# Casting one PSUM bank in two halves, on ScalarE and on VectorE, in a recurrent attention kernel

## The chip, the cores and the metric

The kernel runs on one core of one Trainium2 chip. The metric is the device time of one execution in microseconds (us). The engines are written as the profile writes them: PE is TensorE (PEld its weight loads), ACT is ScalarE, DVE is VectorE, POOL is GpSimd, SP is SyncE.

## The reference

Two branches work on the same x (1 x 2048 x 512, bf16), and a gate mixes them.

```python
g = _sigmoid((x * gate_w).sum(-1, keepdims=True))
a = _A_ref(x, A_mem0, A_Wq, A_Wk, A_Wv, A_Wo, A_seg_len)   # recurrent attention
b = _B_ref(x, B_w1, B_b1, B_w2, B_b2)                      # layernorm, 512 -> 1376 gelu -> 512
return g * a + (1 - g) * b

# _A_ref: 64 segments of 32 tokens, 32 heads of 128, memory of M = 8 tokens
mem = mem0
for s in range(n_seg):
    h = jnp.concatenate([mem, xs], axis=1)                 # 8 + 32 tokens, xs is segment s of x
    q, k, v = (einsum of h with Wq, Wk, Wv)
    p = _softmax(where(mask, q k^T * Dh**-0.5, -1e9))
    o = jnp.einsum('bhqk,bhke->bhqe', p, v)
    o = jnp.einsum('bhte,hed->btd', o, Wo)                 # output projection
    mem = o[:, :M, :].copy()                               # memory of the next segment
    outs.append(o[:, M:, :])
```

The 64 segments are a chain: the first 8 rows of a segment's output projection are the memory that the next segment's q, k and v are made from.

## The kernel before, in words

The kernel has two stages. The first (up to about 110 us) computes the mixer branch b for all tokens, in blocks of 256, stores (1 - g) * b in DRAM, and loads the attention weights, which then stay in SBUF. The second is the loop over the 64 segments, `for s in range(nseg)`, which takes the rest of the time. It is written under a manual schedule: each engine executes its instructions in the order in which the Python code issues them, and the framework adds the semaphore waits that the data dependences ask for.

PSUM has eight banks, each a tile of 128 partitions x 512 f32: U0 to U3 for q and k, and later for the attention output; X1 and X2 for v and for side work; SbF and W for the scores. W serves three purposes in an iteration: half of the scores, then the output projection, then the transposed memory rows.

One iteration s does the following, in this order on PE.

1. Line 110 (`qk_unit`): q and k of the segment into U0 to U3, 64 matmuls from the 32 token columns in `hT`. ACT casts each bank to `Tb` (line 115), and DVE transposes it to `QT` or `KT` (line 119).
2. Lines 254 and 258: scores. Line 129 (`v_unit`): v into X1 and X2. ACT takes the exponentials (line 644) and casts v to `V` (lines 659 and 670). DVE normalises the memory columns (lines 651 and 652).
3. Lines 265 and 268: the sums of the other columns into SbF. DVE takes their reciprocal (line 588, in `recip_x`). Lines 278 and 283 (`av`): attention output into U0 to U3. ACT casts its memory columns to `UT` (line 680), and then the other columns to `XR` (line 583), which POOL normalises in the next iteration (lines 599 and 600).
4. `wo_pass`, the output projection: 32 matmuls of line 141 from `UT` and `Wo_sb` into bank W. Then a cast of W on ACT, line 607, to the bf16 tile `w`, one of 11 buffers of 128 x 512.
5. Line 246 (`mask_mm(0)`): a mask into SbF. Then two units of side work (`run(W3)`).
6. Line 691: four matmuls with `w` as weights, one for each 128 columns of it, which select the memory rows and transpose them; they write columns 0 to 31 of bank W. DVE casts the result to the next `hT` (line 692), and updates a running minimum, `rmin` (line 693). The next iteration starts from `hT`.

The side work is a generator, `side(T, si)`, from which the loop takes units with `run(n)`: q, k and v of the tokens left over from a 128-token tile (`left_qk`, `left_v`), their output projection (`wo_left`), the transpose of the next tile of x (`x_mm`, copied to `xT` by DVE at line 160), and the assembly of finished output rows (`out_sel`, lines 224, 226 and 230), which reads `w` of earlier segments. A few iterations at the start and at the end have little or no side work.

The last segment is finished after the loop. There `wo_pass` is called twice more, first for the segment before the last (pass 64, issued between the reciprocal of line 704 and the multiplies of lines 707 and 708), and then for the last one (pass 65, read by line 732). So there are 65 calls in all, and 63 of them feed line 691.

Of the kernel before, what the change touches and what calls it, by code (L numbers as in the profile page):

```python
# [27 lines left out]
def kernel(ctx, tc, A_x, A_mem0, A_Wq, A_Wk, A_Wv, A_Wo, A_seg_len, B_x, B_w1, B_b1, B_w2, B_b2, gate_w, out):  # L28
    nc = tc.nc
    P = 128  # L30
    _, S, Dm = A_x.shape
# [65 lines left out]
    W = lps.tile([P, 512], FP32)  # L97
# [39 lines left out]
    def wo_group(bk, U_, n):  # L137
        j, ih = HORD[n]
        for c in range(4):
            i = 4 * ih + c  # L140
            nc.tensor.matmul(bk[32 * c:32 * c + 32, :], lhsT=U_[:, j, i, :], rhs=Wo_sb[:, 4 * i + j, :],  # L141
                             start=(n == 0), stop=(n == NW - 1), tile_position=(0, 32 * c))
# [460 lines left out]
    def wo_pass(U_):  # L603
        for n in range(NW):
            wo_group(W, U_, n)
        w = cw.tile([P, Dm], BF16, tag="w", bufs=11, name="w")
        nc.scalar.copy(out=w[:], in_=W[:])  # L607
        return w

    W1, W2, W3 = 2, 2, 2  # L610
    for s in range(nseg):
# [71 lines left out]
        flush(dve_q, 9)  # L683
        prep_q(s + 1)
        w = wo_pass(UT[s % 2])
        if s >= 1:
            ws[s - 1] = w
# [15 lines left out]
    nc.gpsimd.memset(UL[T % 2][:, :, :, LEFT * si:seg], 0.0)  # L703
    nc.vector.reciprocal(out=R[:, nx], in_=SbF[:, 0:32 * NG])
    ws[s - 1] = wo_pass(UT[s % 2])
    Rr = R[:, nx].rearrange("p (i q) -> p i q", q=32)
    nc.vector.tensor_tensor(out=E[:, :, 16:48], in0=E[:, :, 16:48], in1=Rr, op=ALU.mult)
# [16 lines left out]
    nc.vector.tensor_scalar(out=good[:, 0:1], in0=tot[:, 0:1], scalar1=R_MIN, scalar2=None, op0=ALU.is_gt)  # L724
    nc.vector.tensor_scalar(out=good[:, 1:2], in0=tot[:, 1:2], scalar1=RSUM_MAX, scalar2=None, op0=ALU.is_lt)
    wf = wo_pass(UF)
    nc.tensor.matmul(X1[0:1, 0:1], lhsT=good[:, 0:1], rhs=good[:, 1:2], start=True, stop=True)
    bad = okp.tile([1, 1], I32)
# [131 lines left out]
```

## Time and profile before

| what | value |
|---|---|
| median of 3 runs | 828.18 us (827.88 to 828.75) |
| the profiled execution's own time | 827.84 us |
| span of the profile | 826.1 us |
| mean granted PE clock | 0.995 |
| PE busy | 787.2 us |
| ACT busy | 574.1 us |
| DVE busy | 434.8 us |
| POOL busy | 250.1 us |
| line 607, ACT, 65 casts of 128 x 512 | 38.1 us, 585 ns each |
| line 692, DVE, 63 casts of 128 x 32 | 12.1 us, 192 ns each |

The profile is of one execution. Its rows give a group of instructions by line, engine and operation, what it writes and reads (out<-in), and busy time, mean duration and the idle time of the engine ahead of it with what ended that. The view of the waits names who waited for whom, with the total in us, the number of times and the longest. The chain that ended last is followed back from the last instruction, at each step to what released it. Ends of matmuls are modelled, and a matmul row's length includes its way through the array, so successive rows overlap.

### The profile page before, as it was taken

How to read it: one execution, taken by the hardware profiler on the slowest of the kernel's cores; microseconds unless marked ns; L12 is line 12 of the kernel's file. 1: busy time of each engine (PE TensorE's matmuls, PEld its weight loads, DVE VectorE, ACT ScalarE, POOL GpSimd, SP SyncE). 2: the span in 40 equal slices, each digit the busy share in tenths (PEclk: the TensorE clock that was granted, in tenths of full speed). 3: DMA queues.
4: the chain of work that ended last, by engine and by line, in shares of the span. 5: the costliest groups of instructions: out<-in, count | busy, mean ns of one | idle time of the engine just before them, and what ended most of it. 6: DMA issues, size and time to landing. Idle time of an engine off the chain costs nothing.

```text
span 826.1 us, 41283 instructions
## 1 busy us (share of the span) xinstructions
PE 787.2 (95%) x18418; PEld 413.4 (50%) x18418; DVE 434.8 (53%) x1059; ACT 574.1 (70%) x1442; POOL 250.1 (30%) x377
## 2 busy tenths in 40 slices
PE   6898998999999999999999999999999999999997
PEld 4565644545454454544454545454544544454443
DVE  4764445455545455554555555545455555555554
ACT  4554676777777677767676777777676767677763
POOL 3000023333333333333323333333333333323331
PEclk9999999999999999999999999999999999999999
DMA  6995111212121221212121212122111212121111
GB/s 193 406 351 187 34 53 54 62 42 80 55 87 54 68 73 38 79 60 81 60 81 54 70 47 86 54 78 64 66 54 57 81 60 81 54 81 51 60 53 62
DMA packets 38952, 70.42 MB, mean 85 GB/s; under 512 B 3948, under 2 KB 29137, under 8 KB 37233
## 3 DMA queue, kind: packets, MB, share of 16 engines
q1 hardware_dynamic: 38720, 67.59, 23.9%
q8 instruction: 146, 2.39, 1.2%
q14 instruction: 38, 0.30, 0.1%
q0 software_dynamic: 48, 0.13, 0.1%
HBM read 59.06 MB, written 4.45 MB: 77 GB/s over the span
## 4 chain that ended last, share of the span: by engine, by line
PE 85%; ACT 6%; DMA 4%; DVE 2%; issue 1%; SPq 0%; POOL 0%; DVEq 0%; ACTq 0%; POOLq 0%
PE U L110 27%; PE X L129 16%; PE W L141 14%; PE X L110 6%; ACT w L607 5%; PE U L278 3%; PE U L461 3%; PE X L141 3%; DMA c_dr<-ct 3%; PE W L691 2%; PE SbF L455 2%; PE W L455 2%; PE SbF L254 1%; DMA w_sb<-in_B_w_dram 1%; PE U L265 1%
## 5 line engine op out<-in xcount | busy, mean ns | idle before, releaser
L115 ACT CAST Tb<-U 128x512 bf16<-128x512 f32 x258 | 188.6, 756 | 59.1 <-PE U L110 33.3
L599 POOL TENSOR_TENSOR UT<-XR,Rb 128x768 bf16<-128x768 bf16 x63 | 104.9, 1666 | 258.5 <-DMA Rb<-r_dr 212.0
L110 PEld LDWEIGHTS <-hT 128*32 128x32 bf16 x4096 | 103.6, 97 | 109.5 <-DVE hT L692 15.3
L129 PE MATMUL X<-Wv_sb,hT 128*32 128x512 bf16 x2048 | 134.8, 378 | 0.0
L110 PE MATMUL U<-Wq_sb,hT 128*32 128x512 bf16 x2048 | 132.9, 379 | 1.4 <-DVE hT L692 1.4
L110 PE MATMUL U<-Wk_sb,hT 128*32 128x512 bf16 x2048 | 132.7, 379 | 0.0
L119 DVE STREAM_TRANSPOSE QT<-Tb 128x256 f32<-128x256 f32 x128 | 57.0, 446 | 134.7 <-ACT Tb L115 129.6
L141 PE MATMUL W<-Wo_sb,UT 128*32 128x512 bf16 x2080 | 124.5, 380 | 1.2 <-ACT UT L680 1.2
L593 POOL TENSOR_TENSOR racc<-racc,R 128x320 f32<-128x320 f32 x63 | 54.6, 866 | 200.3 <-DVE R L588 196.2
L588 DVE RECIPROCAL R<-SbF 128x256 f32<-128x256 f32 x63 | 110.3, 1751 | 0.5 <-PE SbF L268 0.5
L141 PEld LDWEIGHTS <-UT 128*32 128x32 bf16 x2080 | 55.6, 96 | 56.3 <-issue 16.0
L692 DVE CAST hT<-W 128x32 bf16<-128x32 f32 x63 | 12.1, 192 | 129.7 <-PE W L691 124.9
L583 ACT CAST XR<-U 128x256 bf16<-128x256 f32 x252 | 78.6, 438 | 0.0
L119 DVE STREAM_TRANSPOSE KT<-Tb 128x256 f32<-128x256 f32 x128 | 56.8, 444 | 30.6 <-ACT Tb L115 30.3
L607 ACT CAST w<-W 128x512 bf16<-128x512 f32 x65 | 38.1, 585 | 48.0 <-PE W L141 48.0
L680 ACT CAST UT<-U 128x64 bf16<-128x64 f32 x252 | 35.3, 227 | 43.4 <-PE U L283 43.4
L651 DVE RECIPROCAL R<-U 128x32 f32<-128x32 f32 x126 | 45.0, 357 | 23.2 <-PE U L268 19.0
L129 PEld LDWEIGHTS <-hT 128*32 128x32 bf16 x2048 | 45.1, 95 | 20.8
L461 PE MATMUL U<-w_sb,hTm 128*128 128x512 bf16 (+1 forms) x176 | 53.9, 391 | 1.3 <-DMA w_sb<-in_B_w_dram 1.3
L115 ACT CAST Tb<-X 128x512 bf16<-128x512 f32 x62 | 46.4, 748 | 10.8 <-PE X L110 10.7
L455 PEld LDWEIGHTS <-w_sb 128*128 128x128 bf16 (+1 forms) x352 | 35.3, 104 | 31.1 <-issue 13.6
L265 PEld LDWEIGHTS <-BO 128*32 128x32 bf16 x760 | 29.4, 94 | 34.6 <-issue 14.0
(146 smaller groups left out, 1190.9 us busy)
## 6 DMA issues: line engine op xcount, KB each, us to landing
Rb<-r_dr SPq DMA_DIRECT2D x63, 512.0 KB
Wq_sb<-in_A_Wq_dram SPq DMA_DIRECT2D x4, 1024.0 KB
Wk_sb<-in_A_Wk_dram SPq DMA_DIRECT2D x4, 1024.0 KB
Wv_sb<-in_A_Wv_dram SPq DMA_DIRECT2D x4, 1024.0 KB
Wo_sb<-in_A_Wo_dram SPq DMA_DIRECT2D x4, 1024.0 KB
VP<-VL SPq DMA_DIRECT2D x64, 64.0 KB
xt<-in_A_x_dram SPq DMA_DIRECT2D x16, 128.0 KB
c_dr<-ct SPq DMA_DIRECT2D x16, 128.0 KB
```

The lines of the kernel that those rows point to most:

```text
L110: nc.tensor.matmul(bk[32 * j:32 * j + 32, :], lhsT=G[:, kc, :], rhs=W5[t][:, kc, h0:h1, j, :], start=(kc == 0), stop=(kc == KC - 1), tile_ ...
L115: nc.scalar.copy(out=Tb[:].rearrange("p a e b -> p a b e"), in_=bk.rearrange("p (a b e) -> p a b e", a=8, b=2))
L119: nc.vector.transpose(out=dst[:, 8 * hf:8 * hf + 8, 0:32, :].rearrange("p a r b -> p a (r b)").bitcast(FP32), in_=Tb[:].rearrange("p a e b ...
L129: nc.tensor.matmul(bk[32 * j:32 * j + 32, :], lhsT=G[:, kc, :], rhs=Wv5[:, kc, 4 * vb:4 * vb + 4, j, :], start=(kc == 0), stop=(kc == KC - ...
L141: nc.tensor.matmul(bk[32 * c:32 * c + 32, :], lhsT=U_[:, j, i, :], rhs=Wo_sb[:, 4 * i + j, :], start=(n == 0), stop=(n == NW - 1), tile_po ...
L455: nc.tensor.matmul(hp[:rows, 0:TB * P], lhsT=w1_sb[:, kc, fc * P:fc * P + rows], rhs=yTs[blk][:, kc, :], start=(kc == 0), stop=(kc == KC - 1))
L461: nc.tensor.matmul(bp(blk, tt)[:], lhsT=hTm[blk % 2][:rows, fc, tt * P:(tt + 1) * P], rhs=w2_sb[:rows, fc, :], start=(fc == 0), stop=(fc = ...
L583: nc.scalar.copy(out=XR[:, j], in_=U[j][:, 0:NG * 40].rearrange("p (i q) -> p i q", q=40)[:, :, 8:40])
L588: nc.vector.reciprocal(out=R[:, 8 * NG:], in_=SbF[:, 0:32 * NG])
L593: nc.gpsimd.tensor_tensor(out=racc[:], in0=racc[:], in1=R[:], op=ALU.add)
L599: nc.gpsimd.tensor_tensor(out=UT[(s + 1) % 2][:].rearrange("p j i q -> p (j i) q")[:, :, M:32], in0=XR[:, :, 0:RIDE], in1=Rb[:, :, 0:RIDE] ...
L607: nc.scalar.copy(out=w[:], in_=W[:])
```

## The change

In `wo_pass`, the cast of W to `w` is written as two casts: ACT takes columns 0 to 255, and DVE columns 256 to 511. All 65 passes are concerned. In the changed kernel the second cast is line 608, and all later lines move down by one (691 becomes 692, 692 becomes 693, 707 becomes 708).

```diff
@@ -604,7 +604,8 @@
         for n in range(NW):
             wo_group(W, U_, n)
         w = cw.tile([P, Dm], BF16, tag="w", bufs=11, name="w")
-        nc.scalar.copy(out=w[:], in_=W[:])
+        nc.scalar.copy(out=w[:, 0:Dm // 2], in_=W[:, 0:Dm // 2])
+        nc.vector.tensor_copy(out=w[:, Dm // 2:Dm], in_=W[:, Dm // 2:Dm])
         return w
```

## Prediction

> **What bounds the kernel now.** I read the page first: which engine fills the span, and what the chain that ended last is made of.
>
> ```profile
> span 826.1 us, 41283 instructions
> PE 787.2 (95%) x18418; PEld 413.4 (50%) x18418; DVE 434.8 (53%) x1059; ACT 574.1 (70%) x1442; POOL 250.1 (30%) x377
> ...
> PE 85%; ACT 6%; DMA 4%; DVE 2%; issue 1%; SPq 0%; POOL 0%; DVEq 0%; ACTq 0%; POOLq 0%
> ```
>
> TensorE is the bound: 95% busy and 85% of the chain. The next share, ACT's 6%, is almost wholly the cast that is changed (ACT w L607 alone has 5% in the chain's lines). Then the waits, to see how much of that cast TensorE really stands still for:
>
> ```profile
> DVE hT L692 <- PE W L691: 124.9, 61, 2.3
> PEld L691 <- ACT w L607: 42.1, 63, 1.0
> PE W L691 <- ACT w L607: 11.3, 62, 0.6
> PE U L110 <- DVE hT L692: 1.4, 5, 0.4
> ```
>
> The columns are total us, times, longest. TensorE's matmuls wait for w in every iteration, 11.3 us in all, some 0.16 us each and 0.59 in three iterations that have no other work to put there. This is the largest wait that TensorE has in the loop. VectorE waits for those matmuls about 2 us each time, so it has nothing to do while w is cast. Last, the timeline of one iteration around the cast (start, length, engine; idle before in brackets):
>
> ```profile
> 417.72 0.28 PE L246 MATMUL SbF<-Mk,ident 128*32 128x224 bf16 x4
> ...
> 417.82 0.62 PE L129 MATMUL X<-Wv_sb,GL 128*32 128x512 bf16 x8
> 417.96 0.58 ACT L607 CAST w<-W 128x512 bf16<-128x512 f32 x1 [0.75 <-PE W L141]
> ...
> 418.60 0.25 PE L691 MATMUL W<-SelM,w 128*128 128x8 bf16 x4 [0.16 <-ACT w L607]
> ...
> 418.78 0.62 PE L129 MATMUL X<-Wv_sb,GL 128*32 128x512 bf16 x8
> 418.96 0.19 DVE L692 CAST hT<-W 128x32 bf16<-128x32 f32 x1 [2.16 <-PE W L691]
> 419.06 0.48 DVE L693 TENSOR_TENSOR rmin<-rmin,R 128x320 f32<-128x320 f32 x1
> ```
>
> TensorE covers most of the cast with mask and side matmuls, which end at 418.44, and then stands until 418.60. So a shorter cast can win at most the 0.16 us, 11.3 us over all; a longer one is paid in full, since nothing is left in TensorE's queue to run ahead of L691.
>
> **The wait that the change adds.** The order of the built program shows no instruction moved on TensorE and one added on VectorE: the second half (line 608 there) stands between the reciprocal (in one iteration of four, the copy to xT) and the cast to hT. What it waits for decides the case: not TensorE's last product in W, but ACT's semaphore, at just the count that ACT's own half raises. And the four matmuls of L691 now wait for VectorE, the first of them too: they write bank W, which the second half reads. So the halves do not run side by side; they stand in a row, each with its fixed time, and a hand-over is added.
>
> No row of this trace has the two engines reading one bank at once. At the end of the run they read different banks at once, and run at full pace:
>
> ```profile
> 816.41 0.65 ACT L712 CAST UT<-U 128x256 bf16<-128x256 f32 x2 [0.23 <-PE U L283]
> 816.46 0.76 DVE L712 CAST UT<-U 128x256 bf16<-128x256 f32 x2 [0.56 <-PE U L283]
> ```
>
> Beside this row, the Trainium skill (PSUM — Partial Sum Buffer, the section "PSUM bank collisions raise a hardware error") says that ScalarE and VectorE must be kept apart by a semaphore even when both only read the same bank and different columns of it; W is a single bank of 512 f32 columns. The same page's "Specifications (TRN2)" says that the two read in parallel at full bandwidth where the banks differ, which the row above bears out. By the second sentence alone the sum would be that of the first rival below; by the first it is the sum that follows.
>
> **The cost of a pass.** The L712 rows are the same operation at the halves' size: ACT 372 and 378 ns (375), VectorE 415 and 425 (420), against 585 for the whole cast on ACT (all 65 within 1 ns). The hand-overs are medians over the trace, from the end of one to the start of the other: TensorE's W to ACT 46 ns, ACT to VectorE 32 (Tb to its transpose), VectorE to a waiting matmul 56 (L254), ACT to the matmul 56 (L691).
>
> Before, from the end of W to the first L691: 46 + 585 + 56 = 687 ns. After: 46 + 375 + 32 + 420 + 56 = 929. So 242 ns more, all behind the last matmul that TensorE can do, and its wait grows from 0.16 to about 0.40 us.
>
> Bounds: ACT's half is at most 459 (the longest L583, same size, queued behind others), and 312 if only its pitch counts (four L583 in 1.25 us). VectorE's half is between 345 (start to start of the two L712) and 446 (mean of L119 at this width). Together that is +104 to +352 ns. I take the L712 values, since that row matches in operation, size and types, and since L691 starts 56 ns after the recorded end of w although ACT's next cast began 0.1 us before that end: a hand-over counts from the end, not from the pitch.
>
> Is VectorE free? In all 65 casts, no VectorE instruction of the trace lies in the stretch where the half would run. Behind its wait stand only the cast to hT, which needs L691 anyway, and rmin, which nobody awaits soon. POOL does run there, for 0.1 to 0.2 us mostly; L230, also VectorE out of f32 PSUM, takes 708 to 710 with POOL beside it for most of its length, so I charge nothing. ACT is free 0.21 us earlier, which is worth next to nothing: for its other casts of the loop, UT and V, TensorE waits 1.2 and 1.0 us in the whole run. No DMA, POOL or SP instruction moves.
>
> 63 passes with L691: 63 x 0.242 = 15.2 us.
>
> **The two passes at the end.** Pass 64's cast on ACT starts at 815.59, off the path. But its second half now stands in VectorE's queue ahead of the two multiplies L707 and L708, which ran at 814.80 and 815.15 and are on the chain. The half runs from 815.59 + 0.375 + 0.032 = 816.00; L707 follows 0.345 later, at 816.34, and takes 0.425; L278's first 16 matmuls follow at 816.82 and take 0.20, so L283 starts at 817.02 instead of 815.95: +1.07. (L708 no longer sets it: POOL's L718, beside which it took 753, is over by 815.82, and L652, its like, takes 226.) Pass 65 is on the chain up to L732: +0.24.
>
> **Sum.** 15.2 + 1.1 + 0.2 = 16.6 us against the profiled execution's own 827.84 (span 826.1 and 1.7 around it): 844.4. The median of the runs is 828.18, 0.3 higher, so I say 844.5, 2.0% slower.
>
> **Rivals.** First, **side by side**: VectorE's half starts from TensorE's last product, as its name says. Then W to VectorE 105 ns (L691 to L692) + 420 + 56 = 581 instead of 687: 0.106 less a pass, all inside TensorE's 0.16, so 63 x 0.106 = 6.7 us won; pass 64's half would still delay L707, by some 0.9 less 0.2 that L283 waits already. That makes 828.2 - 6.7 + 0.7 = about 822. For it: the overlap of the L712 rows. Against it: the wait in the built program. It decides only if that wait is over before ACT's half is, and the count says it isn't. 3%.
>
> Second, **the halves overlap in their tails**: if the pitches count, +0.104 a pass, 63 x 0.104 = 6.6 and about 1 at the end: 836. For it: ACT's casts start 0.1 us before the recorded end of the one ahead. Against it: that is inside one engine, while all hand-overs between engines in the trace come after the end. 8%.
>
> Third, **VectorE's half is slowed by POOL**: beside POOL's long operations L652 took up to 812 ns instead of 226. If one pass in four lost 0.53 (753 - 226, as L708 did), 16 x 0.53 = 8.5 more: 853. Against it: L652 and L708 read bf16 in SBUF; L230, out of PSUM, wasn't touched. 5%.
>
> **How the numbers follow.** The forecast, in a row with full hand-overs, has 84%. Its own range is 840 to 850: below, a quarter of the 15.2 us taken back elsewhere in the loop; above, nearly the upper bounds of both halves (63 x 0.352 + 1.4 = 23.6 us, 851.8). That leaves 16% out, so the range is this one. A change under 0.2% (1.7 us) is about what a measurement of this kernel cannot tell from none. Faster: the first rival, 3%. Same: 2%, the low edge of the second. Slower: 95%.
>
> **What would show it.** In the new profile: w twice, near 375 ns on ACT and 420 on VectorE, 65 times each; the VectorE half waiting for "ACT w", not for "PE W"; TensorE's wait at the four matmuls near 0.40 us a pass, 26 us in all, with VectorE's w as releaser; VectorE's w in the chain; L707's twin 1.5 us later. Wrong would be: the two casts with nearly equal starts; a half of over 500 ns; a wait of 0.40 with a total that rises by less than 12 us, which would mean that the loop takes it back.

## The result, and the profile after

The changed kernel takes 842.74 us in the median of four runs (841.41 to 843.62), against 828.34 before. The ratio is 1.0173, with a 95% interval of 1.0155 to 1.0190: slower by 14.4 us. The profiled execution took 843.19 us, 15.35 more than that of before. The ratios here and below are estimates over the runs in the faster of two states, and differ from the quotient of the two medians by 0.14% at most; one run of before, beside the last experiment, took 1533 us and is not in its ratio.

The page of the changed kernel: span, engines, chain by engine, and the groups of the two casts (busy, mean ns of one | idle of the engine ahead, with what ended it).

```profile
span 841.4 us, 41257 instructions
PE 780.9 (93%) x18390; PEld 421.4 (50%) x18418; DVE 459.7 (55%) x1124; ACT 559.9 (67%) x1442; POOL 249.7 (30%) x377
...
PE 85%; ACT 5%; DVE 4%; DMA 3%; issue 2%; SPq 0%; POOL 0%; ACTq 0%; DVEq 0%; POOLq 0%
...
L608 DVE CAST w<-W 128x256 bf16<-128x256 f32 x65 | 27.6, 425 | 94.4 <-ACT w L607 94.4
...
L607 ACT CAST w<-W 128x256 bf16<-128x256 f32 x65 | 24.2, 372 | 48.1 <-PE W L141 48.1
```

ACT is relieved: 574.1 us busy before, 559.9 now. But in the row of VectorE's half the engine idles until "ACT w", in all 65 passes, and the chain has lost one point of ACT and gained two of DVE. The waits of the changed kernel (us in all, times, longest):

```profile
DVE w L608 <- ACT w L607: 94.4, 65, 1.8
...
PE W L692 <- DVE w L608: 20.7, 48, 0.8
...
PEld L110 <- DVE hT L693: 11.4, 47, 0.4
...
PE W L692 <- ACT VL L194: 6.0, 15, 0.4
```

TensorE's idle time at the four matmuls is 20.7 + 6.0 = 26.7 us, where before had 11.3. Fifteen of these waits carry the name of ACT's cast VL: that cast ends within 0.03 us of VectorE's half, and the view names the latest. The first matmul waits for VectorE's semaphore alone. The timeline of one iteration:

```profile
434.26 0.62 PE L110 MATMUL X<-Wk_sb,GL 128*32 128x512 bf16 x8
434.39 0.37 ACT L607 CAST w<-W 128x256 bf16<-128x256 f32 x1 [0.65 <-PE W L141]
...
434.80 0.42 DVE L608 CAST w<-W 128x256 bf16<-128x256 f32 x1 [1.46 <-ACT w L607]
...
435.28 0.24 PE L692 MATMUL W<-SelM,w 128*128 128x8 bf16 x4 [0.40 <-DVE w L608]
```

ACT's half ends at 434.76, VectorE's starts at 434.80 and ends at 435.22, and the matmuls start at 435.28. One after the other, each with its whole length.

### The profile page after: what moved, and what is told of

The parts are those of the page before. It is cut to its first block, busy times and chain, and to the rows that moved or that the text cites. A ratio compares the mean times of both kernels' runs of the same rounds, so it can differ in the third digit from the quotient of the medians.

```text
span 841.4 us, 41257 instructions
## 1 busy us (share of the span) xinstructions
PE 780.9 (93%) x18390; PEld 421.4 (50%) x18418; DVE 459.7 (55%) x1124; ACT 559.9 (67%) x1442; POOL 249.7 (30%) x377
## 4 chain that ended last, share of the span: by engine, by line
PE 85%; ACT 5%; DVE 4%; DMA 3%; issue 2%; SPq 0%; POOL 0%; ACTq 0%; DVEq 0%; POOLq 0%
PE U L110 26%; PE X L129 16%; PE W L141 14%; PE X L110 6%; PE U L278 3%; PE U L461 3%; PE X L141 3%; DVE w L608 3%; ACT w L607 2%; PE W L692 2%; PE SbF L455 2%; PE W L455 2%; DMA c_dr<-ct 1%; PE SbF L254 1%; DMA w_sb<-in_B_w_dram 1%
## 5 line engine op out<-in xcount | busy, mean ns | idle before, releaser
L110 PEld LDWEIGHTS <-hT 128*32 128x32 bf16 x4096 | 106.7, 97 | 105.5 <-DVE hT L693 11.4
L608 DVE CAST w<-W 128x256 bf16<-128x256 f32 x65 | 27.6, 425 | 94.4 <-ACT w L607 94.4
L607 ACT CAST w<-W 128x256 bf16<-128x256 f32 x65 | 24.2, 372 | 48.1 <-PE W L141 48.1
L129 PEld LDWEIGHTS <-hT 128*32 128x32 bf16 x2048 | 45.1, 95 | 20.7
L461 PE MATMUL U<-w_sb,hTm 128*128 128x512 bf16 (+1 forms) x164 | 51.3, 391 | 1.9 <-DMA w_sb<-in_B_w_dram 1.3
```

What stands on the lines that cost most here:

```text
L110: nc.tensor.matmul(bk[32 * j:32 * j + 32, :], lhsT=G[:, kc, :], rhs=W5[t][:, kc, h0:h1, j, :], start=(kc == 0), stop=(kc == KC - 1), tile_ ...
L129: nc.tensor.matmul(bk[32 * j:32 * j + 32, :], lhsT=G[:, kc, :], rhs=Wv5[:, kc, 4 * vb:4 * vb + 4, j, :], start=(kc == 0), stop=(kc == KC - ...
L461: nc.tensor.matmul(bp(blk, tt)[:], lhsT=hTm[blk % 2][:rows, fc, tt * P:(tt + 1) * P], rhs=w2_sb[:rows, fc, :], start=(fc == 0), stop=(fc = ...
L608: nc.vector.tensor_copy(out=w[:, Dm // 2:Dm], in_=W[:, Dm // 2:Dm])
```

## The experiments

Eleven kernels tell the causes apart. Each was compared with the kernel before on the same chip; the median of before there is given, since chips differ by a microsecond or two. "End of W to the first matmul" is measured in the records of the trace, as the median over 63 passes: 687 ns before, 929 in the changed kernel.

**Both halves on ACT.**

```diff
-        nc.scalar.copy(out=w[:], in_=W[:])
+        nc.scalar.copy(out=w[:, 0:Dm // 2], in_=W[:, 0:Dm // 2])
+        nc.scalar.copy(out=w[:, Dm // 2:Dm], in_=W[:, Dm // 2:Dm])
```

> Both halves of W are cast by ACT, one after the other; VectorE is not in it. Theory (the loss is two casts in a row, each paid from its start to its recorded end, with a hand-over between engines): inside one engine the second cast starts before the recorded end of the first (two L712 casts on ACT took 0.65 us together), so from the end of W to the first matmul 46 + 650 + 56 = 752 ns against 687 before and 929 after; +0.065 us a pass, 63 passes, 4 us: about 832 us. Rival A (splitting as such is what costs, each piece with its full 0.37 us): 46 + 372 + 372 + 56 = 846 ns, +10 us: about 838 us. Rival B (nothing but VectorE's presence costs): 687 ns, 828 us.

Measured: 831.59 us against 829.72, ratio 1.0021 (1.0007 to 1.0034). End of W to the first matmul: 745 ns, where 752 was expected and rival A had 846. The casts take 372 and 378 ns, but the second starts 0.27 us after the start of the first. Splitting inside one engine costs 0.058 us a pass, a quarter of what the change costs.

**The whole cast on VectorE** (`nc.vector.tensor_copy(out=w[:], in_=W[:])`).

> The whole of W is cast by VectorE in one piece; ACT is not in it. Theory: one cast, no hand-over between engines in the middle. VectorE took 425 ns for 256 columns and 192 for 32, so 691 for 512; 105 + 691 + 56 = 852 ns from the end of W to the first matmul, 77 less than with the two halves, though VectorE is the slower engine: +0.165 us a pass, 10.4 us, less some 1 us that came back after the matmuls in the changed kernel, and 1.1 us at the end as there: 838 to 839 us, faster than the changed kernel's 842.7. Rival (VectorE's speed or its place in VectorE's queue is the cause, and ACT's half helps): slower than the changed kernel, 845 us or more.

Measured: 839.85 us against 829.72, ratio 1.0108 (1.0082 to 1.0133); 863 ns to the first matmul, where 852 was expected. The cast's row, duration min/median/max:

```profile
L607 DVE CAST w<-W x65: 690/692/692, 118.6 to 832.1; 128x512 bf16<-128x512 f32 x65
```

VectorE alone is 107 ns slower than ACT alone at this cast, and yet faster than ACT and VectorE together by 66 ns. So VectorE's speed is not the cause; the row of two is.

**A small piece for VectorE.**

```diff
+        nc.scalar.copy(out=w[:, 0:448], in_=W[:, 0:448])
+        nc.vector.tensor_copy(out=w[:, 448:Dm], in_=W[:, 448:Dm])
```

> ACT casts 448 columns and VectorE the last 64. Theory (in a row): ACT 532 ns (585 less 64 columns at 0.83 ns each), hand-over 32, VectorE 225 (192 and 32 columns more at 1.04 ns), so 46 + 532 + 32 + 225 + 56 = 891 ns, 38 less than at half and half; 842.7 - 63 x 0.038 = about 840.3 us. Rival (side by side, the time is that of the longer piece): 46 + 532 + 56 = 634 ns, less than the 687 of before: 825 us. Rival (VectorE's time alone sets it): 200 ns less than at half and half, about 830 us.

Measured: 839.05 us against 829.72, ratio 1.0104 (1.0078 to 1.0130); 888 ns, where 891 was expected. Its casts and the wait between them:

```profile
L607 ACT CAST w<-W x65: 532/532/533, 119.1 to 831.3; 128x448 bf16<-128x448 f32 x65
...
L608 DVE CAST w<-W x65: 223/225/226, 119.7 to 831.9; 128x64 bf16<-128x64 f32 x65
...
  ACT w L607: 104.0, 65
```

VectorE's piece fell from 425 to 225 ns and ACT's rose from 372 to 532, and the pass became shorter by their sum, 41 ns. Side by side, ACT's 532 would have been a gain over 585. Most of the small piece is fixed time: 225 ns for 64 columns, where a column costs 1.04 ns.

**Division by partitions.** ACT casts partitions 0 to 63 and VectorE 64 to 127, so that the two pieces have only the bank in common.

> W is divided by partitions: ACT casts partitions 0 to 63, VectorE 64 to 127, each all 512 columns. The two pieces share the bank but no partition. Theory (the wait is set by the bank, whatever part of it is read): in a row, 46 + 585 + 32 + 691 + 56 = 1410 ns, +0.72 us a pass, 46 us: about 874 us. Rival (the wait is set where the two read the same partitions): side by side, 105 + 691 + 56 = 852 ns, about 839 us.

One run: 871.93 us against 829.72; 1409 ns to the first matmul, where 1410 was expected.

```profile
446.05 0.58 ACT L607 CAST w<-W 64x512 bf16<-64x512 f32 x1 [0.65 <-PE W L141]
446.66 0.69 DVE L608 CAST w<-W 64x512 bf16<-64x512 f32 x1 [1.66 <-ACT w L607]
447.41 0.17 PEld L692 LDWEIGHTS <-w 128*128 128x128 bf16 x4 [1.37 <-DVE w L608]
```

The framework's wait goes by the bank, whatever part of it is read (each bank is one tile in this kernel, so the runs do not tell the two apart). The Trainium skill (PSUM — Partial Sum Buffer, "PSUM bank collisions raise a hardware error") allows two engines at once in one bank where their 32-partition quadrants differ. The framework's guard is coarser than that, and whether the chip would have borne it was not tried: there is no run without the wait.

**Two banks, pieces side by side.** Columns 0 to 255 go to bank W and 256 to 511 to bank SbF, which is free once the reciprocal of line 588 has read it; the mask moves behind the four matmuls. Each `wo_half` is four matmuls of 256 columns.

```diff
         for n in range(NW):
-            wo_group(W, U_, n)
+            wo_half(W, U_, n, 0)
+            wo_half(SbF, U_, n, 1)
...
-        nc.scalar.copy(out=w[:], in_=W[:])
+        nc.scalar.copy(out=w[:, 0:Dm // 2], in_=W[:, 0:Dm // 2])
+        nc.vector.tensor_copy(out=w[:, Dm // 2:Dm], in_=SbF[:, 0:Dm // 2])
```

> The output projection writes columns 0 to 255 into bank W and 256 to 511 into bank SbF (64 matmuls of 256 columns in place of 32 of 512, alternating between the banks); ACT casts the one, VectorE the other, into the same tile w. The mask, which goes into SbF, is moved behind the four matmuls. Theory (the wait between the halves comes from the shared bank, not from the shared tile w): VectorE's half waits for TensorE alone, and the casts run side by side: 105 + 425 + 56 = 586 ns from the end of the projection to the first matmul, where before had 687. But the mask's 0.1 us no longer covers any of it, so an iteration is as long as before; with up to 2 us at the end of the run, where pass 64 now waits for the reciprocal that reads SbF, 828 to 832 us where before has 829, if the doubled number of matmuls is free. Rival (the wait comes from w, or from the two engines as such): 929 ns as in the changed kernel, and the mask's 0.1 us on top: some 850 us.

Measured: 873.47 us against 829.00, ratio 1.0533 (1.0510 to 1.0556). The time is a miss, and of a cause that I had placed at the end of the run only:

```profile
435.87 0.29 PE L148 MATMUL W<-Wo_sb,UT 128*32 128x256 bf16 x4
436.83 0.29 PE L148 MATMUL SbF<-Wo_sb,UT 128*32 128x256 bf16 x4 [0.66 <-DVE R L595]
...
438.59 0.37 ACT L615 CAST w<-W 128x256 bf16<-128x256 f32 x1 [1.40 <-PE W L148]
438.70 0.42 DVE L616 CAST w<-SbF 128x256 bf16<-128x256 f32 x1 [1.92 <-PE SbF L148]
```

The first matmuls into SbF come right at the start of a pass, and in every iteration the reciprocal is still reading that bank: TensorE stands 0.96 us into the pass where it would have gone on after 0.1. The loop is 45 us longer for it. What the kernel was made for shows in the last two lines all the same: VectorE's half waits for TensorE and no longer for ACT, and the two casts run at once, though both write the one tile w. The third of the four matmuls, the first that needs VectorE's half, starts 529 ns after the end of the projection, and the first one, for which ACT's half is enough, after 365; 586 was expected for the first. The wait in the changed kernel is the bank's.

**Two banks in sequence.** As the last one, but all matmuls into W come before those into SbF, and ACT casts both halves.

> Two banks as well, but all matmuls of columns 0 to 255 come first (bank W) and then those of 256 to 511 (bank SbF), and ACT casts both halves; VectorE is not in it. Theory (what counts is the stretch from the last product to the last cast's end): the first half is cast while TensorE still works on the second, so 46 + 372 + 56 = 474 ns; with the mask's 0.1 us moved behind, 0.113 less a pass than before, 7 us: 821 to 823 us where before has 829. Rival (the doubled number of matmuls and weight loads costs TensorE more than the cast gives back): each pass longer by more than 0.11 us, 829 us or more.

Measured: 822.24 us against 829.00, ratio 0.9917 (0.9895 to 0.9940), as expected. The mechanism is a little different from the one that I wrote down: the first two of the four matmuls need the first half only and start before the second is cast; but a pass itself is 0.1 us longer than before, 0.06 of it because the first matmul into SbF still waits for the reciprocal.

**320 and 192 columns**, two banks in sequence, both casts on ACT. The later switch leaves the reciprocal time to end.

> As the kernel with two banks in sequence, with 320 columns in the first part and 192 in the second. Theory: ACT takes 318 ns for the last part (585 less 320 columns at 0.83 ns), so 46 + 318 + 56 = 420 ns, just what the two units of side work cover (687 - 160 - 100 = 427); TensorE no longer waits for w at all where there is side work, and the gain is the whole 0.16 us a pass, 10 us: 818 to 820 us where before has 829. Rival (the first part's cast, then 452 less the time to the second part's end, is not done in time, or the matmuls cost more): no better than with halves.

Measured: 816.10 us against 829.00, ratio 0.9849 (0.9829 to 0.9868). This is the fastest complete kernel of the study, faster than the one before and the changed one.

```profile
430.82 1.27 PE L150 MATMUL W<-Wo_sb,UT 128*32 128x320 bf16 x32
...
431.90 0.85 PE L150 MATMUL SbF<-Wo_sb,UT 128*32 128x192 bf16 x32
...
432.13 0.43 ACT L617 CAST w<-W 128x320 bf16<-128x320 f32 x1
432.79 0.32 ACT L618 CAST w<-SbF 128x192 bf16<-128x192 f32 x1 [0.23 <-PE SbF L150]
...
433.11 0.26 PE L701 MATMUL W<-SelM,w 128*128 128x8 bf16 x4
```

The large cast is over while TensorE is still in the pass, and the four matmuls have no idle time ahead of them any more, but for the three iterations without side work (0.8 us in all). It is 2 to 4 us better than was expected, which the last experiment explains.

**The same with VectorE for the second piece.**

> As the kernel with two banks and 320 columns in the first part, with the last 192 columns (bank SbF) cast by VectorE instead of ACT. This is the change's idea, one piece for each engine, without a shared bank. Theory: VectorE waits for TensorE alone and its piece costs 105 + 358 (192 and 160 columns at 1.04 ns) + 56 = 519 ns from the end of the projection, where ACT needs 46 + 318 + 56 = 420; the matmuls that need it wait up to 0.1 us longer, and at the end of the run L707's like stands behind it again, 1 us: 7 us over the 816 of the kernel with ACT in both, about 823 us, still below before's 829. Rival (any cast on VectorE within the pass costs what it did in the changed kernel): 840 us.

Measured: 819.30 us against 828.94, ratio 0.9888 (0.9860 to 0.9915). VectorE's cast, the 358 ns that were expected, waits for "PE SbF L150". It costs 3 us over ACT and not 7: only the later of the four matmuls need it, and 0.043 us a pass is what they are held up. It also starts sooner than was expected, 47 ns after TensorE's last product and not 105. With a bank for each engine, the idea of the change does beat the kernel before.

**The two passes at the end** cast by ACT alone, the loop as in the changed kernel.

> The changed kernel, but the two passes after the loop are cast by ACT alone. Theory: L707's and L708's multiplies no longer stand behind a half, and the last pass has its 0.24 us back: from the end of pass 64's projection to the last output's multiply 5.4 us, as in the kernel before, where the changed kernel has 6.6; the loop keeps its 929 ns a pass: about 1.2 us under the changed kernel. Rival (the end of the run is paced by something else): 6.6 us.

One run: 839.13 us. From the start of pass 64's cast to the last output's multiply it is 5.37 us before, 6.61 in the changed kernel, 5.37 here; the loop has its 929 ns still. These two passes cost 1.24 us. The whole run is 4.1 us under the profiled one of the changed kernel, more than that: its trace also reaches the loop's first group of four matmuls 1.8 us sooner and has a loop 0.8 us shorter, which the edit does not touch and which was not followed up. The changed kernel's end, with pass 64 and L708, which is L707 of before:

```profile
829.20 0.37 ACT L607 CAST w<-W 128x256 bf16<-128x256 f32 x1 [2.67 <-PE W L141]
829.61 0.42 DVE L608 CAST w<-W 128x256 bf16<-128x256 f32 x1 [1.30 <-ACT w L607]
829.95 0.42 DVE L708 TENSOR_TENSOR E<-E,R 128x256 bf16<-128x256 bf16 x1
830.28 0.22 DVE L709 TENSOR_TENSOR E<-E,R 128x64 bf16<-128x64 bf16 x1
830.41 0.28 PE L278 MATMUL U<-E,V 32*128 32x40 bf16 x16 [1.27 <-DVE E L708]
```

The multiply that was ready since 828.3 (the reciprocal's end) starts 0.34 us after the half, as worked out.

**How long TensorE really stands.** Half of the cast is left out; the other half of w is zero.

```diff
+        nc.gpsimd.memset(w[:, Dm // 2:Dm], 0.0)
-        nc.scalar.copy(out=w[:], in_=W[:])
+        nc.scalar.copy(out=w[:, 0:Dm // 2], in_=W[:, 0:Dm // 2])
```

> Only columns 0 to 255 of W are cast, by ACT; columns 256 to 511 of w are set to zero by POOL, so half of the output projection is left out. One bank, 32 matmuls, the mask where it was. The end of W to the first matmul is 46 + 372 + 56 = 474 ns, 213 less than in the kernel before. Theory A (TensorE stands for 0.16 us in a pass of the kernel before, as the profile's idle time says): only 0.16 of the 0.213 can be won, 10 us: 818 us or more where before has 829. Theory B (TensorE really stands for about 0.33 us, because a matmul's row goes on for some 0.165 us after the array can take the next): all of the 0.213 is won, 13.4 us and 0.2 at the end: about 815 us.

Measured: 824.80 us against 828.94, ratio 0.9952 (0.9936 to 0.9968): neither theory, since the edit added a wait of its own.

```profile
428.07 0.37 ACT L608 CAST w<-W 128x256 bf16<-128x256 f32 x1 [0.65 <-PE W L141]
428.32 0.31 POOL L607 MEMSET w<- 128x256 bf16 x1
...
428.50 0.40 PE L692 MATMUL W<-SelM,w 128*128 128x8 bf16 x4
```

The four matmuls start as expected, but take 0.40 us instead of 0.26, because the third needs the zeros, which POOL finishes at 428.63. With the zeros written by VectorE ahead of the pass:

> As left_half_only (columns 256 to 511 of w are zero, half of the output projection is left out), but the zeros are written by VectorE ahead of the pass. In left_half_only the third of the four matmuls waited for POOL's zeros (POOL ended at 428.63, the matmul started at 428.69, 0.19 us after the first), which took back most of the gain. Now all four can start 474 ns after the end of W. Theory A (TensorE stands for 0.16 us in a pass of the kernel before): 10 us won, 818 us or more where before has 829. Theory B (it really stands for about 0.33 us): 0.213 a pass won, 13.4 us: about 815 us.

Measured: 815.29 us against 829.97, ratio 0.9831 (0.9804 to 0.9858). The loop is 12.9 us shorter in the trace, of the 13.2 that 62 times 213 ns make: the 213 ns were won nearly in full. The idle time that the profile shows ahead of the four matmuls fell by less, from 11.3 us to this:

```profile
PE W L692 <- ACT w L608: 1.1, 3, 0.4
```

That is 10.2 us less, where the loop gained 12.9. This is theory B.

## Why the prediction was right, point by point

The direction, the mechanism and the size were right: 844.5 was forecast (840 to 850), 842.74 came.

*The added wait* is what the changed profile shows 65 times. It comes from the bank: not from the shared tile w (two banks), and not from shared partitions (rows). Two reads of W do not depend on each other's data, so this is a wait that the framework adds beyond the data dependences. The Trainium skill's sentence on one bank (PSUM — Partial Sum Buffer, "PSUM bank collisions raise a hardware error") spoke against the change; the runs show only that the framework obeys it, since in none of them do the two casts read one bank at once. The same page's sentence on different banks ("Specifications (TRN2)") is borne out by the casts that overlap in two_banks_side at 372 and 425 ns.

*The cost of a pass* was 929 - 687 = 242 ns by the sum, and 929 and 687 are the measured medians. ACT's half took 372 (375 forecast), VectorE's 425 (420), and the hand-over to the matmul 53 (56); that the sum is exact to the nanosecond is luck, as these small errors cancel. TensorE's idle time at the matmuls went from 11.3 to 26.7 us (26 forecast).

*The 63 passes* were mis-sized: 15.2 us in the sum, 13.5 in the trace (from the first to the last of the four-matmul groups 685.7 us before and 699.0 after, and 0.24 for the first pass). Small things behind the matmuls give 1.8 us back, and the sum had no term for them. The weights of the first matmul are now loaded while VectorE still casts, so the four start within 75 ns instead of 89: 0.9 us. And the cast to hT starts 204 ns after the last of them instead of 271. Before, it had to wait for ACT and for TensorE, and VectorE's queue executed a separate semaphore instruction for that:

```profile
L692 DVEq EVENT_SEMAPHORE  x63: 21/21/21, 119.8 to 805.5; - x63
...
  ACT Tb L115: 4.8, 2
```

The changed kernel, where VectorE itself is the last reader, has none; all_dve, eighth and rows have 204 as well, both_act, where ACT is the last, 273. In most iterations side work covers these 67 ns. They count in four at the start and the end of the loop, 0.3 us, and in two more the gain is larger, 0.7 us together: there, before, the cast to hT stood until ACT's cast Tb (the second line), and now it does not. I had "a quarter of the 15.2 us taken back elsewhere" as the lower edge; an eighth was.

*The two passes at the end*: 1.31 forecast, 1.24 measured.

*The sum*: 16.6 forecast, 13.5 + 1.24 = 14.7 in the parts that the change touches. The rest of the 15.35 between the two profiled executions lies after the last output's multiply (5.11 us before, 5.57 after, 5.35 in tail_whole) and ahead of the loop, and was not followed up.

*A step that was wrong* is "a shorter cast can win at most the 0.16 us, 11.3 us over all". It did not enter the sum of this change, but it set the first rival's cap, and two_banks_320 and left_half_early went through it with 0.20 to 0.21 us a pass. A matmul's row is 379 ns for 512 columns, while the next group of four starts 0.21 us after it; in the rest of the row TensorE could take other work. So an idle time that the profile counts from the end of that row is some 0.16 us shorter than the stand-still. In the iteration of the kernel before that the prediction shows, the last side group started 0.56 us ahead of L691, and TensorE could have gone on 0.35 us ahead of it.

*The rivals.* Side by side did not happen, and could not with one bank and the framework's wait. Overlapping tails exist inside ACT (both_act: 0.27 us from start to start, 372 for the first cast) and not across engines. The first rival also had its hand-over too long: its 105 ns from TensorE to VectorE are those of a cast with two waits, and with TensorE alone to wait for VectorE starts after 47 (two_banks_side, two_banks_dve). POOL slowed nothing: VectorE's half took 424 to 426 ns in all 65 passes.

## What to carry to other kernels

Under this framework, two engines that empty one PSUM bank take turns, whatever they divide: split the bank first, and let the matmuls of the first part end early, so that its cast runs beneath the second. Before you split an operation over two engines, look in the built program for what the second piece waits for; if it is the first piece, add both fixed times and both hand-overs. And read TensorE's idle time as a lower bound of what a shorter wait can win.

## What the runs showed of the hardware

A PSUM cast has a large fixed part on either engine: ACT 319 ns for 192 columns, 372 for 256 (465 in most passes of two_banks_seq, where its row starts 0.19 us before the end of ACT's cast ahead), 532 for 448 and 585 for 512 (0.83 ns a column, some 160 fixed), VectorE 192 for 32, 225 for 64, 358 for 192, 425 for 256 and 692 for 512 (1.04 ns a column, some 160 fixed). Half the partitions cost as much as all: 578 and 694 ns for 64 partitions of 512 columns. A VectorE cast that waits for two engines started 67 to 69 ns later than one that waits for a single one: the cast to hT 271 ns against 204 after the start of the last of the four matmuls, a cast of the projection 116 (all_dve) against 47 (two_banks_side) after TensorE's end.
